# Rank compares on two engines: some of VectorE's key comparisons become signs on ScalarE, and the gates of tiles 12 to 15 run in pairs

## The chip, the cores and the metric

One core of a Trainium2 chip runs the whole kernel. The metric is device time in microseconds; the kernel before takes 315.72 us (median of 3 runs). Engines are named TensorE (PE; its weight loads are PEld), VectorE (DVE), ScalarE (ACT), GpSimd (POOL) and SyncE (SP, which issues most transfers). All of them run at once and wait on each other by semaphores.

## What is computed

Attention with 4 sink positions and a causal window of 128, then a top-1 mixture of 8 experts over its output. Each expert keeps the 80 tokens with the highest gate weight.

```python
# q, k, v: (4, 8, 768, 64)      w_gate: (512, 8)   w1: (8, 512, 1024)   w2: (8, 1024, 512)
keep = is_sink | ((rel >= 0) & (rel < window))          # 4 sinks, window 128
a = softmax(where(keep, 0.125 * q @ k.T, -1e9))
x = (a @ v) as (3072, 512)                              # 3072 tokens
logits = x @ w_gate;  expert_idx = argmax(logits);  gate_w = softmax(logits)[expert_idx]
for e in range(8):
    tok_idx = where(expert_idx == e), the 80 of highest gate_w
    out[tok_idx] = gate_w[tok_idx] * (relu(x[tok_idx] @ w1[e]) @ w2[e])
```

## The kernel before

**Ticks.** The 3072 tokens are 24 tiles of 128. Attention runs in 48 ticks (NTK = 48) and an end (END = 49 and the code behind the loop). A tick treats two pairs of heads for a block of queries: TensorE writes the scores (`scores`, L527), VectorE masks them and takes the maximum (L547, L554), ScalarE takes the exponential with its sum (`exps`, L564), and in the ticks after, TensorE turns the probabilities round (L580), ScalarE copies them out (`keep_probs`, L592), GpSimd masks them (L600, L607) and TensorE multiplies them with the values (L621). The loop at L887 writes out the order of all engines by hand: functions are put into a calendar with `at((tick, stage), f, ...)` and `run` calls them at that stage of the tick. Each engine then takes its own instructions in the order in which they were written.

**Gates.** When a tile's 512 columns are complete, `gate_products` (TensorE, L671) gives its logits, `gate_terms`, `gate_logits`, `gate_hit` and `gate_keys` (VectorE, L681 to L708) its expert and its key. A key is one fp32 number that orders tokens first by expert and then by gate weight: a scale by the expert, a power of two, times the weight. This runs for groups of four tiles up to tile QUADS = 16 and of two from there, and tiles 22 and 23 run alone at the end. `keys_turn` (TensorE, L744) and `keys_keep` (ScalarE, L748) put a group's keys into `krow`, a row of all keys that every partition holds.

**Ranks.** A token's rank is the number of keys that are higher than its own, or equal and earlier. `rank_todo` holds pairs (tile i, piece c) with pieces of 768 columns of `krow`. One `rank_compare` on VectorE compares a piece with tile i's own keys, one per partition, writes 0 or 1 to a buffer `gt` (6 of them, NGT) and the sum over the columns to `parts[:, i, c]`:

```python
    if c0 + w == (i + 1) * P:      # the piece that ends with tile i itself, with ties
        ve.scalar_tensor_tensor(gt, krow[...], keys[:, i:i + 1], ties[...], ALU.subtract, ALU.is_gt, accum_out=ra)
    else:
        ve.tensor_scalar(gt, krow[...], keys[:, i:i + 1], None, ALU.is_ge, ALU.add, accum_out=ra)
```

The comparison serves both ways: TensorE adds up the columns of `gt` (`rank_count`, L779, into row 64 + k of the bank `counts` through a table `pick_row` whose k-th matrix has ones in that column), which says how many later keys fall below each earlier one. At the end of each tick VectorE gets a third of what is in `rank_todo`, rounded up (L928), in ticks 48 and 49 up to three.

**The end.** Behind the loop stand tile 23's gate, its row copy and the last two writes of rows to `x_rows` in DRAM (`rows_write`, L663, in ScalarE's queue; all others are in SyncE's). The last pieces follow, with ScalarE's copy `crow` of the counts (L969), `off` (L974), GpSimd's `ot` and `base` (L977, L987), VectorE's corrections (L989, L996) and the rank sum over `parts` (L1014). From the ranks come the slots (`hot`, L1019), their indices by matmul (`pi`, L1022), the gathers of rows from `x_rows` on GpSimd (L1043) and the expert layers (L1091, L1112). A few matmuls without a use (`keep_warm`) stand between the counts at the end.

**Weights.** 1 MB loads in SyncE's queue (L297) go into buffers as they come free; the first four of the last pool (`wpool3`, L1000) use memory of the attention's buffers. So do the tiles of the last part, `rank` among them, and `rank` waits for what used it last.

## Time and profile before

| what | us |
|---|---|
| median of 3 runs (lowest, highest) | 315.72 (315.42, 317.81) |
| the profiled execution's own time | 313.88 |
| its span in the trace | 312.2 |
| TensorE busy, weight loads busy | 279.8, 222.2 |
| VectorE busy | 177.0 |
| ScalarE busy | 156.0 |
| GpSimd busy | 139.5 |

The busy times are sums over the whole span. The kernel has parts with quite different loads: the ticks, in which all engines work, the end of attention with a chain of small steps, and the expert layers, in which TensorE does nearly everything. What an edit is worth is read from the part in which it stands. Times in the rows below count from the span's start.

### The profile page before, as it was taken

The numbers are of one execution on the slowest core, as the hardware profiler recorded it, in microseconds if no ns is written. First come the engines' busy times: TensorE is split into PE (matmuls) and PEld (weight loads), VectorE is DVE, ScalarE is ACT, GpSimd is POOL, SyncE is SP. The second block draws the span as 40 slices with busy tenths as digits, with TensorE's granted clock in tenths as the row PEclk, the third lists the DMA queues.
The fourth block names the chain that finished last, engine by engine and source line by source line (L and its number), as shares of the span: only waits on it lengthen the run. The fifth ranks groups of instructions, "written<-read, shape, count | busy, mean of one in ns | idle before, by whom it ended". The sixth has DMA issues, their size and how long they took to land.

```text
span 312.2 us, 11461 instructions
## 1 busy us (share of the span) xinstructions
PE 279.8 (90%) x4629; PEld 222.2 (71%) x4631; DVE 177.0 (57%) x533; ACT 156.0 (50%) x620; POOL 139.5 (45%) x337
## 2 busy tenths in 40 slices
PE   7698999999989999999899897858699999999991
PEld 2366777767768687877676675435589998999981
DVE  5865659666677879789999999972020111010001
ACT  1467887887968788787576663100010212021210
POOL 4376784547896467756355645307300110011101
PEclk9679999999999999999999999797689999999998
DMA  6999270899545999778155173983266786768501
GB/s 185 328 314 404 106 249 30 294 294 324 185 163 187 365 377 403 247 243 333 56 164 175 41 305 112 350 315 91 82 205 215 243 314 200 257 240 292 185 23 53
DMA packets 27116, 69.85 MB, mean 224 GB/s; under 512 B 2736, under 2 KB 3760, under 8 KB 26672
## 3 DMA queue, kind: packets, MB, share of 16 engines
q1 hardware_dynamic: 25744, 65.87, 60.6%
q0 software_dynamic: 1024, 2.64, 2.8%
q8 instruction: 39, 0.64, 0.8%
q10 hardware_dynamic: 288, 0.53, 0.4%
q14 instruction: 21, 0.17, 0.2%
HBM read 55.04 MB, written 13.99 MB: 221 GB/s over the span
## 4 chain that ended last, share of the span: by engine, by line
PE 61%; ACT 12%; DVE 12%; DMA 6%; issue 4%; POOL 3%; POOLq 0%; ACTq 0%; SPq 0%; DVEq 0%
PE ph L1091 13%; PE py L1112 12%; PE sc L527 10%; ACT prob L564 9%; PE pp L580 8%; PE xp L621 7%; DVE gt L765 4%; ACT pt L592 3%; DMA x_rows<-xr 2%; PE pl L671 2%; PE pr L655 2%; DMA w<-in_moe_w_dram 2%; PE sc L434 2%; PE bank_t L779 2%; DVE sc L547 1%
## 5 line engine op out<-in xcount | busy, mean ns | idle before, releaser
L564 ACT ACTIVATE prob<-sc,nm 128x132 f32<-128x132 f32 (+1 forms) x192 | 68.9, 377 | 12.3 <-DVE nm L554 12.3
L527 PE MATMUL sc<-kv,q 64*64 64x196 f32 (+2 forms) x768 | 48.8, 342 | 9.7 <-ACT prob L564 7.8
L547 DVE COPY_PREDICATED sc<-upper,sc 128x256 f32<-128x256 int8 x80 | 33.8, 422 | 22.2 <-PE sc L527 10.8
L600 POOL TENSOR_SCALAR_AFFINE_SELECT own<-pt 128x512 f32<-128x512 f32 (+1 forms) x48 | 28.7, 597 | 38.2 <-ACT pt L592 38.1
L592 ACT COPY pt<-pp 128x512 f32<-128x512 f32 x48 | 28.1, 586 | 34.2 <-PE pp L580 23.4
L554 DVE TENSOR_REDUCE nm<-sc 128x2 f32<-128x264 f32 (+1 forms) x96 | 41.4, 431 | 3.3
L1141 POOL DMA_INDIRECT out_dram<-y,idx x8 | 7.4, 921 | 79.4 <-ACT y L1130 68.9
L527 PEld LDWEIGHTS sc<-kv,q 64*64 64x64 f32 x768 | 21.9, 135 | 27.4 <-ACT prob L564 21.0
L564 ACT ACTIVATION_READ_ACCUMULATOR prob<-sc,nm 128x1 f32 x192 | 40.5, 211 | 0.0
L1079 DVE COPY xs<-px 128x320 f32<-128x320 f32 x8 | 3.9, 492 | 61.1 <-PE px L1077 60.7
L621 PE MATMUL xp<-pt,kv 128*64 128x128 f32 x384 | 37.5, 288 | 0.0
L765 DVE TENSOR_SCALAR_CACHE_REDUCE gt<-krow,keys 128x768 bf16<-128x768 f32 x36 | 35.6, 1006 | 0.0
L1091 PE MATMUL ph<-xs,w 128*64 128x80 f32 x704 | 29.4, 244 | 4.3 <-issue 3.0
L580 PE MATMUL pp<-ident,prob 128*128 128x128 f32 x192 | 32.6, 294 | 0.0
L1091 PEld LDWEIGHTS ph<-xs,w 128*64 128x64 f32 x704 | 27.7, 146 | 5.7 <-issue 4.1
L621 PE MATMUL xp<-own,kv 128*64 128x128 f32 x320 | 31.3, 274 | 0.0
L580 PEld LDWEIGHTS pp<-ident,prob 128*128 128x128 f32 x192 | 21.0, 146 | 14.2 <-issue 9.9
L607 POOL TENSOR_SCALAR_AFFINE_SELECT pt<-pt 128x512 f32<-128x512 f32 (+1 forms) x48 | 28.9, 603 | 3.3
L1095 ACT ACTIVATE h<-ph 128x320 f32<-128x320 f32 x16 | 7.0, 438 | 43.5 <-PE ph L1091 43.5
L1112 PE MATMUL py<-h,w 128*64 128x80 f32 x640 | 24.5, 233 | 0.7 <-issue 0.7
L1112 PEld LDWEIGHTS py<-h,w 128*64 128x64 f32 x640 | 23.1, 137 | 1.7 <-issue 1.6
L621 PEld LDWEIGHTS xp<-pt,kv 128*64 128x64 f32 x384 | 21.4, 137 | 3.4
(161 smaller groups left out, 484.3 us busy)
## 6 DMA issues: line engine op xcount, KB each, us to landing
w<-in_moe_w_dram SPq DMA_DIRECT2D x21, 1024.0 KB, 6.6
kv<-in_v_t_dram SPq DMA_DIRECT2D x12, 512.0 KB, 10.2
out_dram<-zeros SPq DMA_DIRECT2D x24, 256.0 KB, 4.1
wkv<-in_moe_w_dram SPq DMA_DIRECT2D x6, 1024.0 KB, 7.4
x_rows<-xr SPq DMA_DIRECT2D x22, 260.0 KB, 2.8
q<-in_q_t_dram SPq DMA_DIRECT2D x11, 512.0 KB, 7.1
kv<-in_moe_w_dram SPq DMA_DIRECT2D x5, 1024.0 KB, 6.0
kv<-in_k_t_dram SPq DMA_DIRECT2D x3, 1584.0 KB, 10.2
```

Source lines behind the costliest of these rows:

```text
L527: pe.matmul(sc[u * D:(u + 1) * D, h, c0 + lo:c0 + hi], qs[g][r, hp, q0:q0 + D], ks[b][r, hp, k0 + lo:k0 + hi], start=True, stop=True, skip ...
L547: ve.copy_predicated(own, upper, sc[:, :, 0:P])
L554: ve.tensor_reduce(out=nm, in_=sc[:, :, lo_c:hi_c], axis=AX.X, op=ALU.max, negate=True)
L564: ac.activation(prob[:, a, h, p0:], sc[:, h, lo_c:hi_c], AF.Exp, bias=nm[:, h:h + 1], scale=1.0, accum_out=ssum[:, n, 2 * hp + h:2 * hp + ...
L580: pe.transpose(pp[:, a, h], prob[:, a, h, SINK:], ident)
L592: ac.copy(pt, st.pop((t, "pp")))
L600: po.affine_select(out=own[:, a0:], in_=pt[:, a0:], pattern=[[0, 2 - a0], [0, 2], [1, P]], compare_op=ALU.is_ge, fill=0.0, base=0, channel ...
L607: po.affine_select(out=pt[:, a0:], in_=pt[:, a0:], pattern=[[0, 2 - a0], [0, 2], [-1, P]], compare_op=ALU.is_gt, fill=0.0, base=0, channel ...
L621: pe.matmul(xp[h * D:(h + 1) * D, a * P:(a + 1) * P], val[:, (2 * hp + h) * D:(2 * hp + h + 1) * D], pr[:, a, h], start=False, stop=(a == ...
L765: ve.tensor_scalar(gt[:, 0:w], krow[:, c0:c0 + w], keys[:, i:i + 1], None, ALU.is_ge, ALU.add, accum_out=ra)
L1091: pe.matmul(ph[fc // (HC // 2)][m * D:(m + 1) * D, fc % (HC // 2)], columns(0, e, c, fc * P + m * D), x[:, c], start=(c == 0 and fc % (HC ...
L1112: pe.matmul(to[m * D:(m + 1) * D, dc], columns(1, e, k, dc * P + m * D), h[:, k], start=(k == 0 and (between is not None or dc == 0)), sto ...
```

## The change

1. **Signs on ScalarE.** A new function `rank_sign` takes a piece that lies wholly ahead of tile i and computes the sign of (1 - 2^-24) * key' + `under`, with its sum, where `under` is 2^-23 times the power of two in key i, less key i: +1 where key' is at least key i, else -1. Results go to two buffers `gts` of their own; GpSimd turns the sum into a count (`sign_settle`, sum/2 + 384) and TensorE counts the columns with a table of halves (`pick_half`). GpSimd also takes 64 per Sign from the constant `later` at the end.
2. **How many.** One Sign at the end of each tick from tick 38 if more than one piece is waiting: 8 in ticks 38 to 46 (none in tick 41) and one each in ticks 48 and 49. Two for the first pieces waiting and two for tile 23 stand behind the loop: 14 in all.
3. **`under`** takes a mask on VectorE in `gate_keys` (from tile 8 on) and two small GpSimd operations (`keys_under`).
4. **VectorE** gets a third of the list, but at most two pieces, in a tick.
5. **QUADS** goes from 16 to 12, so tiles 12 to 15 are two pairs instead of one group of four.
6. `gt` has 5 buffers instead of 6; `pick_row` becomes one wide row read at a shifting place; idle matmuls at the end use other operands and are fewer, since they belong to compares.

```diff
-    PIECE, NPC, NGT = 768, 4, 6
+    PIECE, NPC, NGT = 768, 4, 5
+    BELOW = 1.0 - 2.0 ** -24
...
+            if i0 >= 8:
+                ve.tensor_scalar(under[:, i0:i0 + nb].bitcast(I32), keys[:, i0:i0 + nb].bitcast(I32), 0x7F800000, None,
+                                 ALU.bitwise_and)
+
+        def keys_under(i0, nb):
+            kk, to = keys[:, i0:i0 + nb], under[:, i0:i0 + nb]
+            po.tensor_scalar(to, to, 2.0 ** -23, 1.0, ALU.mult, ALU.mult)
+            po.tensor_tensor(to, to, kk, ALU.subtract)
...
+        def rank_sign(least=0):
+            whole = [n for n, (i, c) in enumerate(rank_todo) if i >= least and c < i * P // PIECE]
+            if not whole:
+                return
+            i, c = rank_todo.pop(whole[0])
+            signed[c] += 1
+            gt = wk.tile([P, PIECE], BF16, tag="gts", name=f"gts_{i}_{c}", bufs=2)
+            ra = parts[:, i, c:c + 1]
+            ac.activation(gt, krow[:, c * PIECE:(c + 1) * PIECE], AF.Sign, bias=under[:, i:i + 1], scale=BELOW, accum_out=ra)
+            sign_new.append((i, c, gt, pick_half))
...
+        def sign_settle():
+            for i, c, gt, pick in sign_new:
+                ra = parts[:, i, c:c + 1]
+                po.tensor_scalar(ra, ra, 0.5, 0.5 * PIECE, ALU.mult, ALU.add)
+                rank_done.append((i, c, gt, pick))
+            sign_new.clear()
...
-        QUADS = 16
+        QUADS = 12
...
+                sign_settle()
+                if len(rank_todo) > 1 and n >= 38:
+                    rank_sign()
                 left = len(rank_todo)
-                for _ in range(min(left, 3) if n >= NTK else -(-left // 3)):
+                for _ in range(min(left, 2 if n < NTK else 3, -(-left // 3) if n < NTK else left)):
                     rank_compare()
...
+            sign_settle()
             rank_count()
             if rank_todo:
                 rank_compare()
+            rank_sign()
+            rank_sign()
             rows_turn(i, 0)
             rows_keep(i, 0)
...
             rank_todo[:0] = held
+            sign_settle()
+            rank_sign(i)
+            rank_sign(i)
             rows_write(i, 0, ac)
...
+            for c, m in enumerate(signed):
+                if m:
+                    j = slice(c * PIECE // P, (c + 1) * PIECE // P)
+                    po.tensor_scalar(later[:, j], later[:, j], 1.0, -0.5 * P * m, ALU.mult, ALU.add)
             po.tensor_tensor(base, later, os, ALU.subtract)
```

The first place is VectorE at the end of tick 44 in the kernel before (`gt_c` is the buffer of piece c; three pieces are tile 17's, the last is tile 18's):

```order
L713 TENSOR_TENSOR onehot<-eq_all,cm_all 128x32
L714 TENSOR_TENSOR ahead<-cm_all,p_bits 128x32
L765 TENSOR_SCALAR gt_0_2919,parts<-krow,keys 128x768
L765 TENSOR_SCALAR gt_1_2921,parts<-krow,keys 128x768
L762 SCALAR_TENSOR_TENSOR gt_2_2923,parts<-krow,keys,ties 128x768
L765 TENSOR_SCALAR gt_0_2925,parts<-krow,keys 128x768
```

and in the changed kernel, up to the reciprocals of the next group:

```order
L724 TENSOR_TENSOR onehot<-eq_all,cm_all 128x32
L725 TENSOR_TENSOR ahead<-cm_all,p_bits 128x32
L773 SCALAR_TENSOR_TENSOR gt_2_2966,parts<-krow,keys,ties 128x768
L776 TENSOR_SCALAR gt_1_2968,parts<-krow,keys 128x768
L650 TENSOR_SCALAR xr_2981,un_2982<-sum_2652 128x2x8
```

Four compares became two; a piece of the list goes to ScalarE in this tick, and others were done in earlier ones.

The second place is ScalarE's queue behind the loop, before: tile 23's gate exponential (`ex`), its row copy (`xr`), the two row writes, the key row and the reads of the counts.

```order
L695 ACTIVATE ex_177<-ls_3300 128x8
L659 COPY xr_3218<-sc_114 128x512
L663 DMA x_rows<-xr_3090 128x520
L748 COPY krow<-sc_113 128x128
L663 DMA x_rows<-xr_3218 128x520
L969 COPY crow<-bank_t 8x384
L974 COPY off<-sc_114 128x8
```

and the same queue in the changed kernel, where `gts` are the buffers of the Signs:

```order
L697 ACTIVATE ex_178<-ls_3356 128x8
L791 ACTIVATE gts_1_3375,parts<-krow,under 128x768
L791 ACTIVATE gts_2_3377,parts<-krow,under 128x768
L661 COPY xr_3268<-sc_114 128x512
L665 DMA x_rows<-xr_3133 128x520
L759 COPY krow<-sc_113 128x128
L791 ACTIVATE gts_0_3410,parts<-krow,under 128x768
L791 ACTIVATE gts_1_3412,parts<-krow,under 128x768
L665 DMA x_rows<-xr_3268 128x520
L1015 COPY crow<-bank_t 8x384
L1020 COPY off<-sc_114 128x8
```

Two Signs came in ahead of the first row write and four ahead of the second and of the two reads.

The third place is VectorE behind the loop, from tile 23's key to the rank sum, before:

```order
L765 TENSOR_SCALAR gt_2_3341,parts<-krow,keys 128x768
L762 SCALAR_TENSOR_TENSOR gt_3_3348,parts<-krow,keys,ties 128x512
L765 TENSOR_SCALAR gt_0_3352,parts<-krow,keys 128x768
L765 TENSOR_SCALAR gt_1_3357,parts<-krow,keys 128x768
L765 TENSOR_SCALAR gt_2_3362,parts<-krow,keys 128x768
L762 SCALAR_TENSOR_TENSOR gt_3_3367,parts<-krow,keys,ties 128x640
L765 TENSOR_SCALAR gt_0_3402,parts<-krow,keys 128x768
L765 TENSOR_SCALAR gt_1_3404,parts<-krow,keys 128x768
L986 TENSOR_REDUCE os<-ot 128x24
L989 TENSOR_TENSOR parts<-parts,sc_113 128x24
L765 TENSOR_SCALAR gt_2_3416,parts<-krow,keys 128x768
L762 SCALAR_TENSOR_TENSOR gt_3_3438,parts<-krow,keys,ties 128x768
```

and in the changed kernel, the rank sum included:

```order
L773 SCALAR_TENSOR_TENSOR gt_3_3415,parts<-krow,keys,ties 128x640
L776 TENSOR_SCALAR gt_2_3456,parts<-krow,keys 128x768
L773 SCALAR_TENSOR_TENSOR gt_3_3458,parts<-krow,keys,ties 128x768
L1032 TENSOR_REDUCE os<-ot 128x24
L1039 TENSOR_TENSOR parts<-parts,sc_113 128x24
L1048 TENSOR_TENSOR parts<-parts,sc_114 128x23
L1066 TENSOR_REDUCE rank<-parts 128x24
```

Ten compares between the key and the rank sum became three.

## Rows read from the trace of the kernel before

**Rows 1.** Busy time by stretch: stretch, length, busy us (xinstructions) of PE, PEld, DVE, ACT, POOL, clock, DMA share, GB/s.

```profile
112.51:134.39 21.88, 21.68 (x329) 17.59 (x325) 18.88 (x48) 17.57 (x75) 17.12 (x32) 1.00 0.92 348
134.39:181.63 47.24, 43.82 (x587) 32.86 (x584) 44.27 (x136) 32.37 (x133) 24.97 (x71) 1.00 0.47 167
181.63:206.28 24.65, 19.66 (x204) 13.18 (x204) 22.79 (x78) 7.91 (x27) 10.50 (x38) 0.93 0.75 275
```

**Rows 2.** Chain of waits in time order: start us, us, what; VectorE's compares.

```profile
187.53 1.87 DVE gt L765 x4
```

**Rows 3.** Page, costliest groups: busy us, mean ns of one, idle before.

```profile
L765 DVE TENSOR_SCALAR_CACHE_REDUCE gt<-krow,keys 128x768 bf16<-128x768 f32 x36 | 35.6, 1006 | 0.0
```

**Rows 4.** Chain of waits, first and last step of a gate group on VectorE.

```profile
182.87 0.21 DVE t L681
...
184.62 0.17 DVE keys L708
```

**Rows 5.** Groups by line and shape, ScalarE, ticks 27 to 46: busy us, mean ns, idle before.

```profile
L564 ACT ACTIVATE prob<-sc,nm 128x132 f32<-128x132 f32 x72 | 26.0, 377 | 5.7 <-DVE nm L554 5.7
L564 ACT ACTIVATION_READ_ACCUMULATOR prob<-sc,nm 128x1 f32 x84 | 17.6, 209 | 0.0
L592 ACT COPY pt<-pp 128x512 f32<-128x512 f32 x21 | 12.3, 587 | 13.4 <-PE pp L580 10.2 <-PE bank_t L585 0.9 <-POOL picks L719 0.9
L631 ACT COPY xt<-xp 128x256 f32<-128x256 f32 x20 | 7.5, 376 | 0.1
```

**Rows 6.** Chain of waits: four Exps with reads; TensorE's steps of one tick.

```profile
132.41 1.43 ACT prob L564 x8
...
154.71 0.45 PE pr L655 x4
...
159.13 0.33 PE bank_t L779 x2
...
160.76 0.89 PE pl L671 x32
...
162.47 0.60 PE pp L580 x4
```

**Rows 7.** Timeline of ScalarE, end: start us, us, engine, line, operation [idle before, releaser].

```profile
193.90 0.21 ACT L695 ACTIVATE ex<-ls 128x8 f32<-128x8 f32 x1 [1.05 <-DVE ls L689]
194.01 0.57 ACT L659 COPY xr<-sc 128x512 f32<-128x512 f32 x1
194.03 0.39 ACTq L663 DMA_DIRECT2D x_rows<-xr  x1
196.01 0.27 ACT L748 COPY krow<-sc 128x128 f32<-128x128 f32 x1 [1.43 <-PE sc L744]
196.07 0.33 ACTq L663 DMA_DIRECT2D x_rows<-xr  x1
201.53 0.47 ACT L969 COPY crow<-bank_t 8x384 f32<-8x384 f32 x1 [5.25 <-PE bank_t L779]
```

**Rows 8.** Timeline of GpSimd and VectorE, end of attention.

```profile
197.48 0.19 POOL L727 TENSOR_TENSOR gr<-gr,g 128x1 f32<-128x1 f32 x1
...
203.63 0.24 POOL L987 TENSOR_TENSOR parts<-later,os 128x24 f32<-128x24 f32 x1 [0.47 <-DVE os L986]
...
206.28 0.30 DVE L1014 TENSOR_REDUCE rank<-parts 128x24 f32<-128x144 f32 x1
```

**Rows 9.** Page, DMA issues: count, KB each, median us to landing.

```profile
x_rows<-xr SPq DMA_DIRECT2D x22, 260.0 KB, 2.8
```

**Rows 10.** Timeline of SyncE, 200 to 206 us.

```profile
203.67 0.37 SPq L297 DMA_DIRECT2D w<-in_moe_w_dram  x1
```

**Rows 11.** Waits of SyncE, 185 to 212 us: total, times, longest.

```profile
SPq L297 <- DMA x_rows<-xr: 8.5, 2, 6.5
```

**Rows 12.** Busy time by stretch, the DMA's share and GB/s last.

```profile
194.00:210.00 16.00, 10.32 (x101) 5.77 (x104) 14.09 (x38) 1.73 (x7) 3.16 (x12) 0.89 0.96 350
194.00:208.00 14.00, 9.25 (x85) 4.97 (x87) 12.93 (x35) 1.49 (x5) 3.16 (x12) 0.88 1.03 375
```

More of the change, by code (lines that the diff above doesn't have):

```diff
@@ L263, in attention_moe @@
     keys = const.tile([P, NTILE], F32, name="keys")
+    under = const.tile([P, NTILE], F32, name="under")
     gate = const.tile([P, NTILE], F32, name="gate")
@@ L310, in attention_moe @@
     ve.memset(zeros, 0.0)
-    first_exp = const.tile([P, 1], F32, name="first_exp")
-    ac.activation(first_exp, zeros[:, 0:1], AF.Exp)
+    ac.activation(under[:, 0:1], zeros[:, 0:1], AF.Exp)
     with ExitStack() as actx:
@@ L366, in attention_moe @@
             ve.memset(t, 0.0)
-        pick_row = const.tile([P, 8, P], BF16, name="pick_row")
+        pick_row = const.tile([P, P + 8], BF16, name="pick_row")
+        pick_half = const.tile([P, P + 8], BF16, name="pick_half")
         def load_q(g, pieces=1):
@@ L483, in make_picks @@
         def make_picks():
-            po.memset(pick_row, 1.0)
-            po.affine_select(out=pick_row, in_=pick_row, pattern=[[-1, 8], [1, P]], compare_op=ALU.is_equal,
-                             fill=0.0, base=-64, channel_multiplier=0)
+            for t, x in ((pick_row, 1.0), (pick_half, 0.5)):
+                po.memset(t, 0.0)
+                po.memset(t[:, D + 7:D + 8], x)
         def read_numbers():
@@ L767, in rank_compare @@
             if min(i * P, c0 + w) > c0:
-                rank_done.append((i, c, gt))
+                rank_done.append((i, c, gt, pick_row))
+        signed = [0] * NPC
+        def rank_sign(least=0):
[8 more added lines that the diff above has]
+            sign_new.append((i, c, gt, pick_half))
+        sign_new = []
+        def sign_settle():
[4 more added lines that the diff above has]
+            sign_new.clear()
         first = [True]
         def rank_count():
-            for i, c, gt in rank_done:
+            for i, c, gt, pick in rank_done:
                 c0, c1 = c * PIECE, min(i * P, (c + 1) * PIECE)
@@ L778, in rank_count @@
                     w = min(c1, (k + 1) * CROW) - c0
-                    pe.matmul(counts[:, c0 - k * CROW:c0 - k * CROW + w], pick_row[:, k], gt[:, c0 - c * PIECE:c0 - c * PIECE + w],
+                    pe.matmul(counts[:, c0 - k * CROW:c0 - k * CROW + w], pick[:, 7 - k:7 - k + P], gt[:, c0 - c * PIECE:c0 - c * PIECE + w],
                               start=first[0], stop=True, skip_group_check=True)
@@ L785, in rank_count_last @@
         def rank_count_last(cnt):
-            for i, c, gt in rank_done:
+            for i, c, gt, pick in rank_done:
                 for j in range(c * PIECE // P, min(i, (c + 1) * PIECE // P)):
-                    pe.matmul(cnt[:, j:j + 1], gt[:, j * P - c * PIECE:(j + 1) * P - c * PIECE], ones_bf[:, 0:1], start=True,
+                    pe.matmul(cnt[:, j:j + 1], gt[:, j * P - c * PIECE:(j + 1) * P - c * PIECE], pick[:, D + 7:D + 8], start=True,
                               stop=True, skip_group_check=True)
@@ L854, in attention_moe @@
                     at((t + kr, "act mid"), keys_keep, q0, qn)
+                    if q0 >= 8:
+                        at((t + kr, "pool"), keys_under, q0, qn)
                 for n in range(nb):
@@ L939, in keep_warm @@
                 for _ in range(times):
-                    pe.matmul(idle_bank, ones_bf, pick_row[:, 0:4], start=True, stop=True)
+                    pe.matmul(idle_bank, ones_bf, ones_bf[:, None, :].to_broadcast([P, 4, P]), start=True, stop=True)
             now[0] = n
@@ L990, in attention_moe @@
             last = misc("last")[:, 0:NTILE]
+            sign_settle()
+            rank_count_last(last)
             while rank_todo:
```

2 lines of the change are left out of this document (added).

## The prediction

> **What bounds the kernel now.** I read three views in this order: the busy time by stretch, the chain of waits in time order, and the timeline of the end of attention. The stretches are cut at the first score maximum of ticks 30, 36 and 47 and at the rank sum, so the second holds 6 ticks, the third 11, the last what follows the last tick's scores [rows 1]. In the 6 ticks TensorE is busy 21.68 of 21.88 us. In the 11 ticks VectorE is busy 44.27 of 47.24 and ScalarE 32.37: a tick is 4.29 us there against 3.65 before. In the last stretch VectorE is busy 22.79 of 24.65 us. So VectorE, with its rank compares, bounds about 72 us of the 312, and the question is which engine or wait bounds them next. A full compare of 768 keys takes VectorE 0.935 us in a row (two compares with their two reads of the sum, in 1.87 us) [rows 2]; there are 36 in the kernel [rows 3].
>
> **What the edits cost and free, engine by engine.** *Ticks 30 to 35.* From the order, VectorE runs 7 full compares instead of 5, because tiles 12 and 13 now come as a pair of their own three ticks sooner: 2 x 0.935 = 1.9 us. A further gate group, priced from its chain (182.87 to 184.79), adds 1.9 us [rows 4]; the masks, priced at the 0.17 us of the key product, add some tenths [rows 4]. VectorE goes from 18.88 to 22.7 us of work in a stretch of 21.88. This stretch gets longer.
>
> *Ticks 36 to 46.* VectorE runs 9 full compares instead of 18: 8.4 us less, 0.7 more for four masks, so 44.27 becomes about 36.5. ScalarE takes 8 compares. None of this form is in the trace. The nearest rows: Exp with a bias column over 132 columns is 0.377 us, its read of the sum 0.209, and four such pairs in a row take 1.43, or 0.358 a pair; the copy of 512 columns takes 0.587 and that of 256 0.376, so a column costs 0.00082 us [rows 5, 6]. 636 more columns are 0.53 us, and a Sign pair is 0.89 us in a row, 1.12 if its read doesn't overlap. I take 0.89, since the Sign stands between other work in the same queue as the Exps do. ScalarE: 32.37 + 8 x 0.89 = 39.5 us. TensorE needs, back to back, per tick (159.13 to 163.07, less 0.33 of counting and 0.89 of gate products) 2.7 us; with six transposes of rows at 0.45, three gate products at 0.89, about 16 counted pieces at 0.33 and the key transposes that is 41 us in both kernels [rows 6]. So three engines that stood at 44, 41 and 32 now stand at 36.5, 41 and 39.5.
>
> A rule stands against moving this work at all. The Trainium skill, "ScalarE: Activation LUTs", section "Rules for kernel authors", sends simple elementwise operations to VectorE, up to about 3x faster per element in bf16. By it a Sign would cost up to 2.8 us and the eight 22 us, and the kernel would be slower. The rows disagree: this fp32 compare with a sum runs at 1.2 ns per column on VectorE [rows 2], ScalarE's copies at 0.82 [rows 5]. The third rival below takes the part of it that the rows leave room for.
>
> *What the ticks come to.* With these prices I summed each tick's work by engine along the printed order. If each tick lasts as long as its busiest engine, the kernel before gives 21.8 us for the 6 ticks and 49.9 for the 11; the trace has 21.88 and 47.24, together 69.1. If whole stretches are bounded by their busiest engine it gives 68.0. So the measured time stands 0.3 of the way up between the bounds 68.0 and 71.7. The changed kernel has 25.2 + 44.9 = 70.1 by ticks and 22.7 + 41.4 = 64.1 by stretches. Three near equal engines wait on each other more than one full one, so I take 0.4 of the way: 66.5, a gain of **2.6 us**, with ends of 5.0 and a loss of 1.0.
>
> *The end of attention.* VectorE drops 7 full compares (6.5 us) and gains three masks of 0.17 [rows 4]: alone, its rank sum would come 6.0 us sooner than 206.28. Two other things then stand in the way. All times of this paragraph are those of the trace before, without the 2.6 us.
> - The sum chain. Crow, the read of the rank counts, is on ScalarE, behind four new Signs and the last row write. ScalarE's queue runs: Exp of the last gate at 194.35 (193.90 now, plus 0.45 for one wider compare and masks on VectorE), 0.21; two Signs, 1.78; row copy 0.57; first row write 0.39; key copy 0.27; two Signs, 1.78; then the last row write at **199.35** instead of 196.07, and crow at 199.7 [rows 7]. From crow to the end of the base sum is 2.34 us now; three new small GpSimd operations on later and two on parts add some 0.6, at 0.19 each for the nearest one and partly overlapped [rows 7, 8]. So the rank sum could start at about **202.7**, 3.6 us sooner.
> - The row write itself. The rank sum's tile lies in memory that the row buffers held, so it waits until the last two row writes have landed; the gathers need them too. Now the last one goes out at 196.07 and lands just before 203.67, where SyncE, which waited for these writes, issues the next weight load: 7.6 us, beside weight loads in flight and a full DMA, against 2.8 for a row write elsewhere [rows 7, 9 to 12]. Today that is 2.6 us before VectorE arrives and costs nothing. At 199.35 + 7.6 it would land at 206.95. The bytes ahead of it bound that: from 194 to 210 the DMA moves 16 us x 350 GB/s = 5.6 MB, of which 1.05 belong to the load issued at 203.67, which in the changed kernel waits for this very write. The other 4.55 MB are through, at the 375 GB/s of 194 to 208, by **206.1** [rows 10, 12].
>
> So this write lands between 202.7, below which the sum chain decides, and 206.95. I take 206.1, since both late writes now wait about as long as the loads ahead of them: the end gains **0.2 us** (between a gain of 3.6 and a loss of 0.7). What follows the rank sum is the same work.
>
> *Edits at nothing.* The smaller pick tables are made by GpSimd in tick 3; its selects for that tick are used by TensorE later, so the cover is TensorE's own tick. The POOL operations that settle a sum (0.19 each) stand where GpSimd is busy 25 of 47 us. Five compare buffers instead of six hold, because at most two compares are issued a tick and counted in the next. Fewer idle matmuls in the end only touch TensorE while it waits. The table load stays one in the printed order.
>
> **The sum.** The profiled execution is 313.88 us, 1.84 under the median of 315.72. 313.88 - 2.6 - 0.2 = 311.1, and beside the median that is **312.9 us**.
>
> **Rivals.**
> - *The last row write lands early.* It goes out 3 us later behind the same loads, so fewer bytes are left ahead of it. Then the sum chain decides: 315.72 - 2.6 - 3.6 = **309.5**. For it: the 2.8 us of other writes; against: both late writes took some 7.5 under load. The Trainium skill's "DMA: Bandwidth & Descriptors", section "Queues, rings and completion order", says that a DMA engine takes the queue rows in turn, a packet at a time; by that the write waits for one packet and not for whole loads, and this rival would hold; the 7.6 us of this trace don't look like it. Chance 0.28.
> - *VectorE's gain in the ticks goes into ScalarE and TensorE.* Ticks at the by-tick bound of 70.1: 315.72 + 1.0 - 0.2 = **316.5**. For it: TensorE's 21.68 of 21.88 in ticks where VectorE didn't bind, and a longer stretch of ticks 30 to 35. Chance 0.18.
> - *ScalarE becomes the bound (the slower side).* A Sign at 1.12 instead of 0.89 adds 8 x 0.23 = 1.8 us in ticks where ScalarE already leads; the next tick's copy of transposed probabilities waits behind it, and the matmuls for that copy. The four Signs ahead of the last row write put that 0.9 later too. From 1.0 us a Sign on ScalarE leads in most ticks. 316.5 + 1.8 + 0.9 = **319.2**. Chance 0.12.
> - The forecast: 0.42.
>
> **How the numbers follow.** A change of over 1% (3.16 us, about what a measurement of this kernel can tell from none) is below 312.56 or above 318.88. Faster: the first rival and 0.16 of the forecast's 0.42 (ticks nearer to 64.1, or a write that lands a little sooner), 0.44. Slower: most of the third, 0.10. Same: 0.46. The forecast's own range is 311.0 to 315.5. The range for 8 in 10 reaches into the first rival and past the second: 309.0 to 318.3; left out are a third of the first and most of the third.
>
> **What would show it.** A Sign over 768 columns at 0.85 to 1.0 us. VectorE busy about 36 us in 11 ticks that last 43 to 45, and ticks 30 to 35 lasting 23 or more. In the last stretch, the last row write issued some 3 us later after the last tick than now, and VectorE idle 3 to 5 us ahead of the rank sum with this DMA as what ended it. If VectorE is not idle there, the first rival holds; if the pairs of Sign and read take over 1 us and TensorE waits for ScalarE's copies, the third. The forecast is wrong above all if TensorE and ScalarE overlap in the ticks better or worse than the trace shows where VectorE bounds them.

## The result, and the profile after

The changed kernel takes 313.31 us (median of 16 runs, 308.86 to 316.01) and the kernel before, run beside it, 317.79 (16 runs, 313.86 to 320.13): a ratio of **0.986** (95% interval 0.982 to 0.990). In a second comparison, on another chip (below), it was 0.997 (0.992 to 1.001). Forecast: 312.9 beside 315.72, a ratio of 0.991, which stands between the two. Ratios, here and below, are of the runs within 1.5% of the fastest of their kernel on that chip, so they need not equal the quotient of the medians. Runs of one kernel differ by some 2 to 3%, and two profiles of one kernel differ by 3 us in the expert layers (below), so the change is read from the stretches of attention, which come back within 0.03 us in the ticks.

The stretches of the changed kernel, cut at the same instructions as [rows 1] (first maximum of ticks 30, 36 and 47, and the rank sum); columns as there:

```profile
113.22:138.68 25.46, 24.46 (x342) 18.71 (x339) 22.15 (x63) 18.97 (x78) 17.64 (x36) 1.00 0.86 325
138.68:181.02 42.34, 41.02 (x569) 31.16 (x568) 36.39 (x118) 37.91 (x148) 27.09 (x82) 1.00 0.50 165
181.02:203.87 22.85, 18.00 (x200) 12.25 (x198) 16.94 (x68) 13.31 (x39) 13.82 (x54) 0.91 0.75 272
```

The six ticks grew from 21.88 to 25.46 us, the eleven fell from 47.24 to 42.34, the end fell from 24.65 to 22.85. From tick 30 to the rank sum that is 3.1 us less. In the eleven ticks VectorE, TensorE and ScalarE now stand at 36.39, 41.02 and 37.91 us: TensorE leads. In the six ticks TensorE's own busy time grew with the stretch, from 21.68 us [rows 1] to 24.46.

What came of the new work on ScalarE is in the groups by line and shape (busy us, mean ns of one, idle before):

```profile
L791 ACT ACTIVATE gts<-krow,under 128x768 bf16<-128x768 f32 x14 | 13.2, 943 | 0.2 <-POOL under L719 0.2
L791 ACT ACTIVATION_READ_ACCUMULATOR gts<-krow,under 128x1 f32 x14 | 2.8, 200 | 0.0
```

The timeline of ScalarE at the end shows what the Signs hold up, beside [rows 7]:

```profile
194.08 0.93 ACT L791 ACTIVATE gts<-krow,under 128x768 bf16<-128x768 f32 x1
194.33 0.41 ACTq L665 DMA_DIRECT2D x_rows<-xr  x1
194.91 0.19 ACT L791 ACTIVATION_READ_ACCUMULATOR gts<-krow,under 128x1 f32 x1
195.00 0.92 ACT L791 ACTIVATE gts<-krow,under 128x768 bf16<-128x768 f32 x1
195.83 0.18 ACT L791 ACTIVATION_READ_ACCUMULATOR gts<-krow,under 128x1 f32 x1
195.92 0.56 ACT L661 COPY xr<-sc 128x512 f32<-128x512 f32 x1
196.39 0.26 ACT L759 COPY krow<-sc 128x128 f32<-128x128 f32 x1
196.87 0.94 ACT L791 ACTIVATE gts<-krow,under 128x768 bf16<-128x768 f32 x1 [0.23 <-POOL under L719]
197.21 0.33 ACTq L665 DMA_DIRECT2D x_rows<-xr  x1
...
198.85 0.47 ACT L1015 COPY crow<-bank_t 8x384 f32<-8x384 f32 x1
```

A Sign starts 0.92 us after the one ahead of it (194.08 and 195.00). The two row writes (ACTq) don't wait for what stands ahead of them in ScalarE's queue to end: the first goes out while the first Sign runs, before the second Sign (195.00) and the row copy (195.92) have begun, the second at 197.21, 0.34 us into the third Sign and ahead of the fourth. On VectorE two waits appear where [rows 8] had none:

```profile
200.58 0.35 DVE L1032 TENSOR_REDUCE os<-ot 128x24 f32<-128x192 f32 x1 [1.90 <-POOL ot L1023]
...
203.87 0.30 DVE L1066 TENSOR_REDUCE rank<-parts 128x24 f32<-128x144 f32 x1 [2.14 <-DMA x_rows<-xr]
```

The rank sum waits 2.14 us for the last row write and for nothing else: the wait that the prediction named. Behind it a small loss came in. The stretch from the rank sum to the first turn of gathered rows (`px`), in the kernel after and, in the second fence, before:

```profile
203.87:213.53 9.66, 7.58 (x39) 4.49 (x40) 3.75 (x9) 0.34 (x2) 3.69 (x4) 0.50 0.65 227
```

```profile
206.28:214.89 8.61, 6.56 (x42) 3.35 (x39) 3.48 (x9) 0.34 (x2) 3.16 (x3) 0.80 0.45 156
```

TensorE's granted clock is 0.50 through the whole stretch, the lower of its two levels (1.2 and 2.4 GHz); before, it was 0.80 on average, and the stretch 1.05 us shorter. What TensorE did in the changed kernel ahead of it, while VectorE waited:

```profile
198.00:200.00 2.00, 0.66 (x7) 0.47 (x6) 0.67 (x2) 1.46 (x4) 1.86 (x9) 0.99 1.03 366
200.00:202.00 2.00, 2.00 (x28) 0.91 (x25) 0.66 (x3) 0.00 (x0) 1.60 (x7) 0.50 1.04 421
202.00:203.87 1.87, 0.31 (x1) 0.00 (x0) 0.00 (x1) 0.00 (x0) 0.00 (x0) 0.50 1.03 413
```

It was busy 0.66 of 2.00 us, the granted clock fell to 0.50, and it had one matmul in the 1.87 us of the wait. What then holds up `px` is a row of 14 matmuls without a use (`warm`) that stands ahead of it in TensorE's queue; the kernel after and, in the second fence, before:

```profile
207.97 5.76 PE L1093 MATMUL warm<-hot 128*80 128x480 bf16 x14 [0.70 <-ACT tab L1086]
```

```profile
210.15 4.68 PE L1041 MATMUL warm<-hot 128*80 128x480 bf16 x14 [0.70 <-ACT tab L1034]
```

At the lower clock they take 1.08 us more. The first gathered rows are taken up 8.31 us after the rank sum (212.18), as against 8.13 before (214.41), but `px` starts 1.35 us behind that instead of 0.48. So some 0.9 of the 1.05 us are these matmuls.

### The profile page after: what moved, and what is told of

The parts are those of the page before. It is cut to its first block, busy times and chain, and to the rows that moved or that the text cites. A ratio compares the mean times of both kernels' runs of the same rounds, so it can differ in the third digit from the quotient of the medians.

```text
span 309.8 us, 11500 instructions
## 1 busy us (share of the span) xinstructions
PE 278.3 (90%) x4622; PEld 221.5 (71%) x4622; DVE 167.1 (54%) x521; ACT 168.2 (54%) x650; POOL 143.0 (46%) x372
## 4 chain that ended last, share of the span: by engine, by line
PE 59%; ACT 13%; DVE 13%; issue 5%; DMA 4%; POOL 3%; SPq 1%; POOLq 0%; ACTq 0%; DVEq 0%
PE ph L1143 13%; PE py L1164 12%; ACT prob L566 8%; PE sc L529 8%; PE pp L582 6%; PE xp L623 6%; ACT pt L594 3%; DVE gt L776 3%; PE pl L673 2%; DMA vst_raw<-in_vs_t_dram 2%; DMA x_rows<-xr 2%; PE warm L1093 2%; DVE sc L549 2%; PE pr L657 1%; DVE nm L556 1%
## 5 line engine op out<-in xcount | busy, mean ns | idle before, releaser
L602 POOL TENSOR_SCALAR_AFFINE_SELECT own<-pt 128x512 f32<-128x512 f32 (+1 forms) x48 | 27.8, 578 | 37.2 <-ACT pt L594 37.1
L556 DVE TENSOR_REDUCE nm<-sc 128x2 f32<-128x264 f32 (+1 forms) x96 | 41.4, 431 | 3.3
L1143 PE MATMUL ph<-xs,w 128*64 128x80 f32 x704 | 28.7, 241 | 4.0 <-issue 2.8
L1143 PEld LDWEIGHTS ph<-xs,w 128*64 128x64 f32 x704 | 26.9, 144 | 5.4 <-issue 3.8
L776 DVE TENSOR_SCALAR_CACHE_REDUCE gt<-krow,keys 128x768 bf16<-128x768 f32 x22 | 21.9, 1004 | 0.0
```

The costliest lines, as they stand in the source:

```text
L556: ve.tensor_reduce(out=nm, in_=sc[:, :, lo_c:hi_c], axis=AX.X, op=ALU.max, negate=True)
L602: po.affine_select(out=own[:, a0:], in_=pt[:, a0:], pattern=[[0, 2 - a0], [0, 2], [1, P]], compare_op=ALU.is_ge, fill=0.0, base=0, channel ...
L776: ve.tensor_scalar(gt[:, 0:w], krow[:, c0:c0 + w], keys[:, i:i + 1], None, ALU.is_ge, ALU.add, accum_out=ra)
L1143: pe.matmul(ph[fc // (HC // 2)][m * D:(m + 1) * D, fc % (HC // 2)], columns(0, e, c, fc * P + m * D), x[:, c], start=(c == 0 and fc % (HC ...
```

## The experiments

All stretches, in us, are read from the profiles in the same way, one profile a row; "rank wait" is VectorE's wait for the last row write ahead of the rank sum. Ratios are to the kernel before on the same chip.

| kernel | ticks 30-35 | ticks 36-46 | tick 47 to rank sum | rank wait | rank sum to px | px to end | ratio (95%) |
|---|---|---|---|---|---|---|---|
| before | 21.88 | 47.24 | 24.65 | 0 | 8.61 | 97.31 | 1 |
| before, again (e8) | 21.87 | 47.26 | 24.66 | 0 | 8.55 | 94.08 | |
| changed | 25.46 | 42.34 | 22.85 | 2.14 | 9.66 | 96.27 | 0.986 (0.982-0.990) |
| changed, again (e9) | 25.48 | 42.37 | 24.17 | 3.83 | 9.20 | 99.73 | 0.997 (0.992-1.001) |
| four-tile gates to tile 16 (e1) | 22.03 | 43.13 | 24.56 | 4.05 | 9.22 | 98.51 | 0.976 (0.970-0.982) |
| row writes early (e2) | 25.46 | 42.34 | 23.28 | 1.64 | 8.79 | 98.50 | 0.986 (0.980-0.992) |
| no Signs at the end (e3) | 25.48 | 42.36 | 23.43 | 0 | 8.52 | 97.56 | 0.989 (0.981-0.996) |
| before, gates in pairs (e4) | 24.36 | 44.06 | 24.72 | 0 | 8.57 | 98.13 | 0.990 (0.982-0.997) |
| loads held back (e5) | 25.49 | 42.37 | 20.88 | 0 | 12.28 | 94.48 | 1.008 (1.004-1.012) |
| e1 and e5 together (e6) | 22.04 | 43.10 | 21.16 | 0 | 12.34 | 96.44 | 0.989 (0.985-0.994) |
| Signs from tick 30 (e7) | 23.94 | 40.92 | 24.27 | 3.95 | 9.48 | 89.31 | 0.975 (0.966-0.985) |
| no limit of two (e10) | 24.58 | 42.45 | 24.25 | 3.92 | 8.83 | 97.83 | 0.987 (0.982-0.992) |
| e1 and e7 together (e11) | 22.25 | 43.08 | 23.05 | 2.19 | 8.79 | 98.09 | 0.982 (0.976-0.987) |
| e7, one load held back (e12) | 23.95 | 40.92 | 24.41 | 3.85 | 8.97 | 98.07 | 0.981 (0.977-0.986) |

The ticks hardly vary between profiles of one kernel (0.03 us). The last three columns of times do: the end by 1.3 us with the landing of the write, the expert layers by 3 and more. So verdicts on the ticks rest on the first two columns.

### Where the six ticks lost 3.6 us

The changed kernel's ticks 30 to 35, one by one, columns as above:

```profile
113.22:117.64 4.42, 4.42 (x82) 3.98 (x79) 3.10 (x9) 3.55 (x14) 3.79 (x9) 1.00 1.04 417
117.64:122.13 4.49, 4.49 (x54) 3.36 (x53) 4.31 (x13) 3.53 (x14) 3.03 (x6) 1.00 1.00 399
122.13:127.21 5.08, 4.70 (x53) 3.10 (x53) 4.84 (x17) 3.40 (x13) 3.56 (x8) 1.00 0.95 362
127.21:129.75 2.54, 1.97 (x32) 1.18 (x32) 2.47 (x6) 2.07 (x11) 0.76 (x3) 1.00 0.65 221
129.75:134.60 4.85, 4.80 (x82) 3.93 (x79) 3.50 (x9) 3.41 (x14) 4.36 (x8) 1.00 0.47 138
134.60:138.68 4.08, 4.08 (x52) 3.17 (x51) 3.91 (x12) 3.01 (x13) 2.14 (x7) 1.00 1.01 384
```

VectorE's work is 22.15 us in 25.46, but it comes in lumps: 4.84 and 2.47 us in the third and fourth tick (5.08 and 2.54 us long), where TensorE is idle for 0.95 us. In the other four ticks TensorE is busy for all but 0.05 us. Its 24.46 us are 2.78 more than before, with 13 more matmuls: mainly four more counts, four more transposes of rows and two more of keys. Five experiments took it apart.

**e1.** The pairs undone:

```diff
-        QUADS = 12
+        QUADS = 16
```

> The changed kernel with four-tile gate groups up to tile 16 again, as before; Signs and the limit of two stay. Theory A (VectorE bounds ticks 30 to 35 because the pair of tiles 12 and 13 brings a gate group and two full compares there): these six ticks fall from 25.5 us to 21.9, as before the change; ticks 36 to 46 take the work back, VectorE 36.4 + 2 x 0.94 + 1.9 = 40.2 us of work, and last about 45 instead of 42.3. Net 0 to 1.7 us faster than the changed kernel, 309 to 311.5 of device time in a profile like that of the changed kernel (311.6). Rival B (the pairs were needed for the Signs to help): ticks 36 to 46 go back to 47 and the kernel is 1 us slower than the changed one. Rival C (ticks 30 to 35 are longer for another reason, such as the masks of the keys or the smaller number of compare buffers): they stay above 24.

Measured: 22.03 and 43.13 us. The times of theory A hold for the six ticks, and the eleven gave back only 0.8 of the 2.7 expected: 65.16 us for all 17 ticks instead of 67.80. That VectorE alone is the cause doesn't follow, since the edit takes TensorE's busy time in the six ticks back as well (21.84 us in this run). The rank wait grew to 4.05, so the rank sum came 0.9 us sooner after tick 30 than in the changed kernel's first profile and 2.3 sooner than in its second (89.72 against 90.65 and 92.02). The ratio is 0.976.

**e4.** The pairs alone, in the kernel before (16 to 12 there):

> The kernel before with gates in pairs from tile 12 on, and nothing else of the change. Theory A (pairs only move VectorE's work from ticks 36 to 46 into ticks 30 to 35): the six ticks grow by about 3 us from 21.9, the eleven shrink by 3 to 3.8 from 47.2, and the time is that of the kernel before within 0.7 us. Rival B (the pairs are a pure cost, in ticks that TensorE fills, and all of the gain is the Signs'): 2 us slower or more. Rival C (the pairs bring most of the gain by themselves): 2 us faster or more.

Measured: 24.36 and 44.06, together 0.7 less than before. Theory A in size, but the six ticks show that it isn't only VectorE's work that moves:

```profile
112.56:136.92 24.36, 24.15 (x344) 19.09 (x341) 23.01 (x64) 19.18 (x78) 17.72 (x32) 1.00 0.93 345
```

TensorE is busy 24.15 of 24.36 us, 2.47 more than before: the counts and transposes of tiles 12 and 13 come into these ticks too. So 2.5 of the 3.6 us are there without any Sign or limit. Without Signs the pairs are worth 0.7 us, with Signs they cost 2.6: the eleven ticks that they relieve were no longer VectorE's. The ratio of 0.990 is more than 0.7 us, but the profile shows no such gain in attention (93.14 against 93.77 from tick 30 to the rank sum).

**e7.** Signs from tick 30:

```diff
-                if len(rank_todo) > 1 and n >= 38:
+                if len(rank_todo) > 1 and n >= 30:
```

> The changed kernel with a Sign per tick from tick 30 on instead of 38: five Signs more in ticks 30 to 35, four full compares fewer there on VectorE (7 to 3), one fewer after. Theory A (VectorE bounds ticks 30 to 35 since the pairs): they fall from 25.5 us to 22.5 to 23.5, ticks 36 to 46 stay at 41.5 to 42.5, so 2 to 3 us less in the ticks; at the end up to 2 us of it is lost again to the wait for the row write. Rival B (TensorE and ScalarE bound these ticks, and a Sign only moves the wait): 25 us or more, no gain.

Measured, the first two stretches:

```profile
112.98:136.92 23.94, 23.77 (x340) 18.55 (x337) 19.08 (x57) 22.44 (x86) 18.64 (x40) 1.00 0.92 343
136.92:177.84 40.92, 40.73 (x572) 31.29 (x570) 35.69 (x117) 37.59 (x148) 27.30 (x82) 1.00 0.50 175
```

VectorE falls from 22.15 to 19.08 us in the six ticks and TensorE is now busy 23.77 of 23.94 and 40.73 of 40.92: these are TensorE's ticks. The fall is 1.5 us there, a little less than theory A said, and 1.4 in the eleven, more than it said. VectorE's load is worth these 1.5 us of the six ticks; the 1.9 down to e1's 22.03 are TensorE's own work. ScalarE holds five more Signs without a loss, so rival B is out.

**e11.** Both e1 and e7:

> Signs from tick 30 and four-tile gates up to tile 16. Theory A (where the Signs start and how the gates are grouped are two cures of the same thing, VectorE's load in ticks 31 to 33): ticks 30 to 35 at TensorE's 21.7 to 22.1 us, ticks 36 to 46 at 43.1, together 65.0 as with either alone (65.2 and 64.9), and the time as with either alone. Rival B (the two add up): together 62.5 or less.

Measured: 22.25 and 43.08, together 65.33, as with either alone (65.16 and 64.86). Theory A: they don't add up. In all three runs TensorE is busy for 64.2 to 64.5 us of the 17 ticks, so with either edit its work is what is left as a bound; in the changed kernel it was busy for 65.48 of 67.80.

**e10.** The limit of two taken out:

```diff
-                for _ in range(min(left, 2 if n < NTK else 3, -(-left // 3) if n < NTK else left)):
+                for _ in range(min(left, 3) if n >= NTK else -(-left // 3)):
```

> The changed kernel without the limit of two compares a tick on VectorE (a third of the list, rounded up, as before). Seven Signs in ticks 38 to 46 instead of eight, as many full compares on VectorE within one. Theory A (the limit spreads VectorE's work and is neutral in sum): ticks 30 to 46 within 0.7 us of 67.8. Rival B (the limit pushes compares of ticks 30 and 31 behind the next pair's gates, which is why the changed kernel has 25.5 us in ticks 30 to 35 where pairs alone gave 24.4): those ticks fall to 24.4 to 24.7 and the eleven stay, 1 us faster. Rival C (it is needed against ticks with four compares): 1.5 us slower or more.

Measured: 24.58 and 42.45, rival B to the letter in the ticks. The first two stretches:

```profile
113.86:138.44 24.58, 24.33 (x344) 19.09 (x341) 23.40 (x65) 19.20 (x78) 18.26 (x36) 1.00 0.94 351
138.44:180.89 42.45, 40.83 (x569) 31.00 (x568) 36.77 (x121) 37.26 (x146) 26.94 (x81) 1.00 0.49 172
```

The limit costs 0.8 us in the ticks; it defers compares into the ticks in which the next pair's gates are due: in the third tick VectorE has 4.84 us of work with the limit and 3.67 without. So the 3.6 us of the six ticks are 2.5 from the pairs (e4), 0.9 from the limit, and 0.2 from the rest of the change.

### What bounds the end

**e2.** The last two row writes ahead of the Signs:

```diff
-            rank_sign()
-            rank_sign()
             rows_turn(i, 0)
             rows_keep(i, 0)
+            rows_write(i - 1, 0, ac)
+            rows_write(i, 0, ac)
+            rank_sign()
+            rank_sign()
...
-            rows_write(i - 1, 0, ac)
...
-            rows_write(i, 0, ac)
```

> The changed kernel with tile 23's row copy and both last row writes ahead of the two Signs for the pieces of tile 22 in ScalarE's queue; all else the same. Theory A (the issue time of the last row write decides when the rank sum starts): the write goes out some 2 us earlier (about 195.1 instead of 197.2 on the changed kernel's axis), VectorE's wait for it ahead of the rank sum (2.14 us) falls to 0 to 0.5, the sum chain, some 0.3 later, decides, and the kernel is 1.5 to 2.0 us faster than the changed one. Rival B (the write lands when the weight loads ahead of it are through, whenever it was issued): it lands where it did, VectorE still waits about 2 us, and the time is that of the changed kernel within 0.5.

Timeline of this kernel, ScalarE's issues and VectorE's rank sum:

```profile
195.63 1.05 ACTq L665 DMA_DIRECT2D x_rows<-xr  x2
```

```profile
205.61 0.30 DVE L1066 TENSOR_REDUCE rank<-parts 128x24 f32<-128x144 f32 x1 [1.64 <-DMA x_rows<-xr]
```

Both writes were out by 196.7, 14.4 us after tick 47's first maximum (182.33), as against 16.5 in the changed kernel (197.21 and 0.33), and the last landed 23.3 after it, as against 22.8 and 24.2 in the changed kernel's two profiles. Issued 2.1 us earlier it took some 9 us. Rival B as to the last write's issue time. The edit left the first of the two writes where it was, 13.3 us after tick 47's first maximum in both kernels; what that means for the landing comes out behind e12.

**e3.** The four Signs behind the loop taken out, their pieces on VectorE:

```diff
-            rank_sign()
-            rank_sign()
             rows_turn(i, 0)
...
-            rank_sign(i)
-            rank_sign(i)
```

> The changed kernel without the four Signs behind the loop; VectorE does these four pieces. Theory A (the end is bounded by the row write, which the Signs delay): VectorE has 3.7 us more, the write goes out 1 to 1.8 us earlier, and from tick 47's first maximum to the rank sum it takes 22.5 to 23.2 us as against 22.85 now: no change, within 0.5 us of the changed kernel. Rival B (the Signs shorten the end by what they take off VectorE): 3.7 us less its idle time, so 1.5 to 3.7 us slower than the changed kernel.

Measured: 23.43 us and no wait for the write, beside 22.85 and 24.17 with the four Signs. VectorE does 3.7 us more and nothing is lost that can be told from the spread of the write. That is a little over theory A's 23.2 and far from rival B. Here VectorE arrives last, but only just: SyncE's load that waits for the same writes goes out at 202.90, 0.32 us ahead of the rank sum at 203.22. These four Signs bring nothing that shows as long as the write lands that late.

**e5.** What decides its landing? The load that waits for the writes goes first of four, so that three loads aren't in flight beside them:

```diff
-        homes += [(wpool3, m) for m in range(NC)]
+        pre = [wpool3.tile([P, 2 * F], F32, tag=f"w{m}", name=f"wp3_{m}", bufs=1) for m in range(NC)]
+        homes += [(None, pre[m]) for m in (3, 0, 1, 2)]
```

> The changed kernel with the four weight loads behind the attention in another order: the one whose memory is free only when the last two row writes have landed goes first, so that the other three (3 MB) queue behind it instead of being in flight beside the writes. Theory A (the writes land when the loads beside them are through): the last write lands 2.5 to 4.5 us after its issue instead of 6.6, VectorE's wait ahead of the rank sum (2.14 us) goes, the sum chain decides and tick 47's first maximum to the rank sum takes 20.8 to 21.5 us instead of 22.85; 1 to 2 us faster than the changed kernel, less what the gathers lose to the loads that now run beside them (0 to 1 us). Rival B (the landing of a row write takes some 7 us there by itself, whatever runs beside it): still 22.5 or more, no change, or slower by the later loads.

Timelines of this kernel: ScalarE's last write, SyncE's first load behind it, VectorE's rank sum and its wait for the first gather:

```profile
198.02 0.33 ACTq L665 DMA_DIRECT2D x_rows<-xr  x1
```

```profile
200.14 2.74 SPq L299 DMA_DIRECT2D wp<-in_moe_w_dram  x4
```

```profile
202.74 0.30 DVE L1067 TENSOR_REDUCE rank<-parts 128x24 f32<-128x144 f32 x1
...
214.54 0.76 DVE L1128 TENSOR_TENSOR xg<-xg 80x256 f32<-80x256 f32 x2 [7.68 <-DMA xg<-x_rows,idx_in]
```

Without the three loads the write lands at most 2.1 us after its issue, not 6.6 (in e6 below again 2.1, from 195.17 to 197.29). The wait is gone and the end takes 20.88 us: theory A, and here the sum chain decides, 2.0 us before the changed kernel. But the four loads then run beside the gathers: the first gather is waited for 7.68 us instead of 4.20, a loss of 3.5 where 0 to 1 was expected, and the kernel isn't faster than before (medians 311.2 and 311.8, ratio 1.008). **e6**, the same with e1's gates:

> The same order of the four loads, with four-tile gates up to tile 16. By theory A of the loads the wait of 4.05 us that the run with four-tile gates showed ahead of the rank sum goes, and tick 47's first maximum to the rank sum takes 20.5 to 21.5 us instead of 24.6: 2.5 to 4 us faster than the run with four-tile gates alone, less up to 1 us in the gathers, so 306 to 308.5. By rival B no change to it, 309 to 311.

Measured: 21.16 us at the end, 3.4 less than e1, and a gather wait of 7.74: the stretch to px is 3.1 longer than in e1. The median was 306.3 us beside 311.84 before, a ratio of 0.989, where e1 alone, on another chip, had 0.976. The gain at the write is given back at the gathers.

**e12.** One load held back, with Signs from tick 30 (order 0, 1, 3, 2):

> Signs from tick 30, and the weight load that waits for the row writes is third of the four instead of fourth, so one load (1 MB, 2.5 us at 400 GB/s) leaves the company of the writes and runs after them. By the theory that the writes land when the loads beside them are through: the last write lands 2 to 2.5 us sooner, VectorE's wait ahead of the rank sum falls from 3.95 to about 1.5 to 2, tick 47's first maximum to the rank sum from 24.3 to 21.9 to 22.5. The gathers start 4.5 us after the rank sum, when the two loads behind are nearly through, and wait within 0.7 us of 4.2 (where all three loads held back cost them 3.5): 1.5 to 2.3 us faster than Signs from tick 30 alone. Rival: the first gather waits as much longer as the write lands sooner, and nothing is gained.

Missed. The wait stayed at 3.85 us. Busy time by stretch (DMA share and GB/s are the last two columns), and VectorE's rank sum:

```profile
198.00:200.00 2.00, 2.00 (x29) 1.07 (x28) 0.66 (x3) 0.00 (x0) 1.91 (x9) 0.59 1.05 422
200.00:202.00 2.00, 0.49 (x2) 0.00 (x0) 0.00 (x0) 0.00 (x0) 0.00 (x0) 0.50 0.74 294
202.00:204.00 2.00, 0.00 (x0) 0.00 (x0) 0.24 (x1) 0.00 (x0) 0.00 (x0) 0.50 0.00 0
```

```profile
203.76 0.30 DVE L1067 TENSOR_REDUCE rank<-parts 128x24 f32<-128x144 f32 x1 [3.85 <-DMA x_rows<-xr]
```

Hardly a byte moves after 202, and yet the write counts as landed only at 203.7, 8.2 us after its issue at 195.51. The load that was held back was the third, and without it the write landed no sooner.

What the write waits for is in the counts by DMA queue. ScalarE's queue, which carries only the two row writes here, is q10, SyncE's is q1 (packets, MB, share of the 16 DMA engines); the changed kernel from 198.0 to 203.4 us and, in the second fence, e5 from 198.8 to 199.7:

```profile
q1 hardware_dynamic: 536, 1.61, 77.1%
q10 hardware_dynamic: 288, 0.53, 25.6%
```

```profile
q10 hardware_dynamic: 144, 0.27, 77.6%
```

In the changed kernel all of both writes (0.53 MB) moves in this stretch, at about 100 GB/s, beside loads that have three quarters of the DMA. Ahead of it, from the first write's issue at 194.33 to 198.2, only the loads move: 3.9 us. In e5 the last write starts alone 0.8 us after its issue and moves in 0.9. So most of the time from issue to landing is a wait for the first packet and a shared DMA. The first packet comes 17.2 us after tick 47's first maximum in the changed kernel, 17.6 in e2 and e12 and 17.0 in the kernel before; the last write stands behind the first in its queue, so in e2 it went out earlier for nothing. Why the first packet comes that late beside loads isn't shown: taking the third load away (e12) didn't change it.

From the last packet of q10 to the moment at which the waiters go on it is 0.5 us in e5 and in the changed kernel's first profile, and 1.1 to 1.2 in its second and in e12, where the last packet is a small one at 202.5. The Trainium skill's "DMA: Bandwidth & Descriptors", section "Anatomy of one DMA — SWDGE (gpsimd) path", puts most of a transfer's fixed 2 us into the receipt of the last byte's write; that is said of GpSimd's path. On ScalarE's queue the 0.5 to 1.2 us measured here are less.

### The same kernels again

> The kernel before once more, for a second profile: which stretches vary from run to run. If the stretches of attention (21.9, 47.2 and 24.65 us) come out within 0.3 us again, differences of a microsecond between kernels in them are the kernels'; what varies is then the expert layers or the start.

> The changed kernel once more, beside the next three on one chip. Attention's stretches within 0.3 us of 25.5, 42.3 and 22.9 us; what differs in the time is the expert layers (98.8 to 108.8 us so far between the rank sum and the end).

Measured: ticks within 0.03 us for both kernels; the changed kernel's end 24.17 instead of 22.85 us, well beyond the 0.3 that was expected, all of it in the wait for the write (3.83 instead of 2.14). The expert layers took 94.08 instead of 97.31 and 99.73 instead of 96.27 us, the one way and the other. TensorE's timeline at the first expert of the kernel before, in the first profile and, in the second fence, in the other:

```profile
216.17 2.45 PE L1091 MATMUL ph<-xs,w 128*64 128x80 f32 x53 [0.58 <-DVE xs L1079]
219.00 0.23 PE L1091 MATMUL ph<-xs,w 128*64 128x80 f32 x1 [0.38 <-issue]
219.72 0.37 PE L1091 MATMUL ph<-xs,w 128*64 128x80 f32 x4 [0.48 <-issue]
221.13 0.55 PE L1091 MATMUL ph<-xs,w 128*64 128x80 f32 x4 [1.05 <-issue]
222.56 4.69 PE L1091 MATMUL ph<-xs,w 128*64 128x80 f32 x66 [0.88 <-issue]
```

```profile
217.50 4.65 PE L1091 MATMUL ph<-xs,w 128*64 128x80 f32 x128 [0.59 <-DVE xs L1079]
```

The same 128 matmuls take 11.1 us in one profile and 4.65 in the other; in the gaps TensorE waits for nothing that the trace shows. Behind the gaps the granted clock is 0.50, in the first profile (columns as in [rows 1]):

```profile
218.62:222.56 3.94, 1.15 (x10) 0.65 (x9) 0.00 (x0) 0.00 (x0) 2.58 (x5) 0.83 0.50 140
222.56:224.90 2.34, 2.34 (x35) 2.33 (x36) 0.00 (x0) 0.00 (x0) 0.00 (x0) 0.50 0.07 28
```

The last 66 matmuls take 4.69 us there. At the other profile's pace they would take about 2.4 (an estimate: 66 of its 128 in 4.65), so some 2.3 of the 6.4 us are the lower clock and the rest the gaps. By the end of the kernel 3.2 of the 6.4 are left (97.31 against 94.08). That is more than the change is worth, so ratios of kernels whose attention differs by a microsecond can scatter by it; how far it makes up the differences of the table isn't shown.

## Why the prediction was right, and where its steps were off

- **The Sign's price held.** 0.89 us a pair in a row was taken from the Exps and copies [rows 5, 6]; the trace has 0.92. The rule of the Trainium skill, "ScalarE: Activation LUTs", section "Rules for kernel authors", that simple work such as `max` or `add` belongs on VectorE gives its factor of up to about 3 for bf16. The estimate of up to 2.8 us that the prediction drew from it doesn't hold for this fp32 compare with a sum: VectorE takes 0.935 us [rows 2] for the same piece.
- **The engines' sums held in the eleven ticks, and for VectorE in the six.** In the eleven VectorE, TensorE and ScalarE were put at 36.5, 41 and 39.5 us and measured 36.39, 41.02 and 37.91; the stretch, put between 41.4 and 44.9, took 42.34. In the six, VectorE was put at 22.7 and had 22.15.
- **TensorE's work in the six ticks was put at nothing more.** The pairs were priced for VectorE alone, and the lower bound of 64.1 us counts 22.7 for the six ticks. TensorE had 24.46 there, of which the pairs bring 2.47 (e4), so the bound by stretches is 24.46 + 41.02 = 65.48.
- **The way between the bounds was off in the six ticks.** "I take 0.4 of the way" for all 17 together gave 66.5 us; they took 67.80, a gain of 1.3 and not 2.6. The eleven came near 0.3 of the way, but the six took 25.46, above even the 25.2 that came from summing each tick's busiest engine. Beside the missing TensorE work, VectorE's heavy ticks held up TensorE for 0.95 us, which then needed its full time in the next. e1 shows the size: without the pairs 2.6 us less in the ticks. The 0.4 itself was an estimate, and its starting point is not in the rows: the 68.0 us of the kernel before are a sum of prices, where the busy times of [rows 1] give 21.68 + 44.27 = 65.95. From there the measured 69.1 is 0.55 of the way to 71.7, and 0.55 of the way from 64.1 to 70.1 is 67.4.
- **"An end of attention that the last row write decides" was right**, the step on which the forecast stood against its first rival: the rank sum waited for it, 2.14 and 3.83 us where 3.4 had been worked out, and e5 and e6 confirm that it decides: with the write early the wait is gone and the sum chain is last. The first rival's early landing is what they show once the loads beside the write are gone.
- **Its issue time was mis-sized.** "Then the last row write at 199.35 instead of 196.07", 3.3 us later after tick 47: it went out 1.75 later (16.19 against 14.44), since a write in ScalarE's queue goes out while Signs ahead of it still run or have yet to begin. That had little weight, because moving the last write's issue didn't move the landing (e2).
- **The byte bound gave about the right time for a reason that is only partly right.** The write was put at 24.5 us after tick 47's first maximum (206.1 on the axis of before); it landed 22.8 and 24.2 after. But the write doesn't wait until the loads ahead of it are through: from 198.2 on its packets move between theirs with a quarter of the DMA, and one load less left the landing where it was (e12). That the time came out is in part luck.
- **"What follows the rank sum is the same work" was right for the work and wrong for the clock**: 0.6 to 1.05 us more to px, for the most part 14 matmuls without a use at a granted clock of 0.50.

In sum: -1.3 in the ticks and -1.8 or -0.5 at the end (two profiles), +1.05 or +0.6 behind it, so 1.1 to 2.1 us less up to px, where 2.8 had been worked out. The medians fell by 4.5 and 2.3 us; where the other 2.4 and 1.1 us lie isn't shown, since between two profiles of one kernel the expert layers differ by over 3 us and the time ahead of tick 30 by up to 1.4. The forecast of the time lies between the two ratios although the ticks gained half of what it gave them, the end more and the stretch behind it lost: that these offset each other is luck. Of the change's parts, the Signs in the ticks carry the gain: with the limit, and gates as before, they take 4.0 us out of the ticks (e1 against before). The pairs take 2.6 of it back and the Signs behind the loop bring nothing that shows.

The versions that did better than both kernels: gates as before (e1, 0.976), Signs from tick 30 (e7, 0.975), and both (e11, 0.982, beside 0.997 for the changed kernel on the same chip). From tick 30 to px they take 98.94, 98.61 and 97.17 us, as against 102.38 before and 100.31 and 101.22 in the changed kernel. e1 and e7 were not run beside the changed kernel, and e7's profile has 89.31 us behind px, 4.8 less than the shortest other, which nothing in its edit explains; on another chip its ticks with one load held back (e12) had 0.981.

## To carry to other kernels

When work moves off the engine that bounds a stretch, cost every tick for itself and not the stretch, and every engine that the edit touches (the pairs brought TensorE's work forward too): an edit that was worth 0.7 us while one engine bound everything (the pairs) cost 2.6 once another did. Look for the wait that stands next behind a chain that is shortened, and ask what its end depends on: here a small write beside large loads, whose issue could be moved by 2 us for nothing while the write ahead of it in the queue stayed. Taking the loads away from it moved the wait to the next small transfer that they then ran beside.

## What the runs showed of the hardware that had not been expected

- A row write of 260 KB lands at most 2.1 us after its issue when no loads run beside it (e5, e6) and 6.6 to 9 us after beside 1 MB loads. There the first packet of the two writes came 3.9 us after the first was issued, and their 0.53 MB then moved in 5 us with a quarter of the DMA. Between the last packet and the moment at which its waiters go on 0.5 to 1.2 us pass.
- A DMA in ScalarE's queue is issued while activations ahead of it still run or have yet to begin: 0.25 us after a Sign of 0.93 us began, with another Sign and a copy between the two in the queue.
- The first 128 matmuls of the expert layers take 4.65 us in some executions of one program and 11.1 in others, with gaps that nothing in the trace explains and, behind them, a granted clock of 0.50. The cause of the gaps stays open.
